# Fused attention and two MoE layers on one core: loading q and k of the first group ahead of need, and adding the mask with a matmul

## The chip, the core and the metric

The kernel runs on one core of a Trainium2 chip. The metric is the device time of one execution in microseconds (us). Five engines work side by side, each through its own instructions in program order: TensorE (PE; its weight loads are listed as PEld), VectorE (DVE), ScalarE (ACT), GpSimd (POOL) and SyncE (SP), which here issues most of the DMA transfers.

## The reference

```python
# attention: 4 batches, 8 heads, 576 positions, 64 channels a head
scores = scale * np.matmul(q, k.transpose(0, 1, 3, 2))
mask_plain = (rel >= 0) & (rel < window)                       # window 32, heads 0-3
mask_dil = (rel >= 0) & (rel < window * dilation) & (rel % dilation == 0)   # dilation 4, heads 4-7
scores = np.where(masks[None, :, :, :], scores, -1000000000.0)
scores = scores - np.max(scores, axis=-1, keepdims=True)
attn = np.exp(scores)
attn = attn / (np.sum(attn, axis=-1, keepdims=True) + 1e-09)
x = np.matmul(attn, v)            # then (4*576, 512) tokens
# first MoE layer, d_ff 2048
h = x @ w_in
y = (h - np.tanh(h)) @ w_out
# second MoE layer, d_ff 1024
h = y @ w_in2
solu = h * softmax(h)
out = (layer_norm(solu) * g_ln) @ w_out2
```

Weights arrive as 64-bit floats, 512 KB for each chunk of 128 rows.

## The kernel before

The 2304 tokens are cut into six groups of 384. Attention for a group is eight *units*; a unit is two heads of two blocks of 96 queries, each against 128 keys. A unit passes through these steps: `qk` (four matmuls into a PSUM tile `qkp`), `then()` of `qk_f32` (DVE adds the mask, takes the row maximum `nm` and writes the masked scores to SBUF as `p`, one instruction for each of four blocks), `sm_exp` (ACT, four exponentials), `sm_norm` (two tiny DVE instructions on the row sums, `rs`, and one POOL multiplication), `tr` (PE transposes `p` into `tp`, ACT copies it to `pt`) and, for two units at a time, `pv` (PE times v; ACT and DVE write the result as a rounded part and a rest, `x`). Units 0 to 21 are computed in full fp32 by `qk_f32`; later units use split operands (`qk_half`) and are not touched.

Each weight chunk is loaded raw (`w_load`) and turned into a rounded part and a rest by `w_step`, a pipeline over four calls: per call one ACT scaling `wa`, one ACT cast `wi`/`wo`, and four DVE instructions (`wi` L85, `wy` L93, L101, L105). There are 32 chunks of the first layer, w_in and w_out.

The program has a *prologue*, rounds r = 0 to 10, for units 0 to 7 of group 0. In round r, PE gets qk of unit r, pv of units r-4 and r-3 (even r), tr of unit r-2; then comes a `w_step` if r is in `SW`, the maximum and exponentials of unit r, the normalisation of unit r-1. Loads are issued by SP in program order; the tile `qkr` that holds q and k of a unit has two buffers, so that the load of unit r+2 waits until PE has read unit r. PSUM tiles `qkp`, `tp` and `pv` have two buffers each in the prologue.

The *main loop* follows: for step s (group g, chunk c of 16), `mm1` computes h in 12 matmuls, tanh, subtraction and split follow on ACT and DVE, and `mm2` adds chunk s-5 to y in 12 matmuls. Attention units of the next groups are put into half-steps (slots) by `plan`: qk of unit u at slot p, its exponentials at slot p+1, its transpose some slots later. They share the PSUM pool `a_ps`, two banks for all of `qkp`, `tp` and `pv` there. `w_step` calls fill the first 42 slots, by the rule with `W0`, `WA`, `WB`. A tile's bank is given to the next tile once all readers of the old one are done. The second layer follows after group 5.

Of the kernel before, what the change touches and what calls it, by code (L numbers as in the profile page):

```python
# [15 lines left out]
B, H, S, D = 4, 8, 576, 64  # L16
# [5 lines left out]
NQ, NK = 96, 128  # L22
NU = 8
QC, KC = 4 * NQ, 4 * NK
# [5 lines left out]
YT = 256  # L30
LAG = 5
WA, WB = 26, 40
SW = range(1, 11)
W0 = 11


@with_exitstack
def tile_kernel(ctx: ExitStack, tc: tile.TileContext, qk, vw, cst, w_in, w_out, w_in2, w_out2, g_ln, out):
    nc = tc.nc
    ctx.enter_context(tc.manual_schedule())  # L40

    const = ctx.enter_context(tc.tile_pool(name="const", bufs=1, side="left"))
    cv_p = ctx.enter_context(tc.tile_pool(name="cv", bufs=2, side="left"))
    wi_p = ctx.enter_context(tc.tile_pool(name="wi", bufs=1, side="left"))
    wo_p = tc.alloc_tile_pool(name="wo", bufs=1, side="left")
    g_p = ctx.enter_context(tc.tile_pool(name="g", bufs=2, side="right"))
    x_p = ctx.enter_context(tc.tile_pool(name="x", bufs=2, side="right"))
    at_p = tc.alloc_tile_pool(name="at", bufs=2, side="right")
# [1 line left out]

    y_dr = dr_p.tile([128, KD, NTOK], F32, name="y_dr")

    cst_sb = const.tile([128, 128 + 3 * NK], F32, name="cst_sb")
    ident = cst_sb[:, 0:128]
    masks = cst_sb[:NQ, 128:].rearrange("p (t k) -> p t k", t=3)

    def mask_of(u, j):

        g, r = divmod(u, NU)
        hp, bp = divmod(r, 2)  # L60
        if hp < 2:
            return 0 if (4 * g + 2 * bp + j) % 6 == 0 else 1
        return (0, 2, 1)[g % 3]
# [46 lines left out]
    wi, wo = [None] * NF, [None] * NF  # L110
# [7 lines left out]


    xt, un = {}, {}  # L120
    NFU = 22

    def load_unit(u):
        if u < NU * NG:
            r = at_p.tile([128, QC + KC], F32, tag="qkr", name=f"qkr{u}")
            n = 64 if u < NFU else 128
            nc.sync.dma_start(out=r[:n], in_=qk[u, :n])
            v = at_p.tile([NK, 2, 2, D], F32, tag="v", name=f"v{u}", bufs=6)
            nc.sync.dma_start(out=v.rearrange("p b h d -> p (b h d)"), in_=vw[u])
            un[u] = dict(r=r, v=v)  # L130

    def prep_unit(u):
        if not NFU <= u < NU * NG:
            return []
        r = un[u]["r"]
        s = at_p.tile([128, QC + 2 * KC], F32R, tag="qks", name=f"qks{u}", bufs=1)
        un[u]["s"] = s
        return [
            lambda: nc.vector.tensor_copy(out=s[:, 0:QC + KC], in_=r),
            lambda: nc.vector.tensor_tensor(out=s[64:128, 0:QC], in0=r[64:128, 0:QC],  # L140
                                            in1=s[64:128, 0:QC].bitcast(F32), op=ALU.subtract),
            lambda: nc.vector.tensor_tensor(out=s[:, QC + KC:], in0=r[:, QC:],
                                            in1=s[:, QC:QC + KC].bitcast(F32), op=ALU.subtract),
        ]

    def new_p(u):
        d = un[u]
        d["p"] = at_p.tile([NQ, 4, NK], F32, tag="p", name=f"p{u}", bufs=3)
        for t in ("nm", "sm", "rs"):
            d[t] = at_p.tile([NQ, 4], F32, tag=t, name=f"{t}{u}")  # L150

    def qk_f32(u, pool, tag):

        d = un[u]
        new_p(u)
        ps = pool.tile([128, 512], F32, tag=tag, name=f"qkp{u}")[:NQ, 0:KC].rearrange("p (b k) -> p b k", b=4)
        for b in range(4):
            nc.tensor.matmul(ps[:, b], d["r"][:64, b * NQ:(b + 1) * NQ],  # L158
                             d["r"][:64, QC + b * NK:QC + (b + 1) * NK], start=True, stop=True)

        def then():
            for b in range(4):
                nc.vector.tensor_tensor_reduce(  # L163
                    out=d["p"][:, b], in0=ps[:, b], in1=masks[:, mask_of(u, b % 2)], op0=ALU.add, op1=ALU.min,
                    scale=-0.125, scalar=3.0e38, accum_out=d["nm"][:, b:b + 1])
        return then

    def qk_half(u, hf, pool, tag):
# [26 lines left out]
    def sm_exp(u, bs=range(4)):  # L195
        d = un[u]
        for b in bs:
            nc.scalar.activation(out=d["p"][:, b], in_=d["p"][:, b], func=AF.Exp, scale=-1.0,  # L198
                                 bias=d["nm"][:, b:b + 1], accum_out=d["sm"][:, b:b + 1])

    def sm_norm(u):
# [42 lines left out]


    st_ps = tc.alloc_tile_pool(name="st_ps", bufs=2, space=PSUM, side="left")
    load_unit(0)
    nc.sync.dma_start(out=cst_sb, in_=cst)
    load_unit(1)
    w_load()  # L250
    load_unit(2)
    for _ in range(3):
        w_load()
    back = None
    for r in range(NU + 3):
        t = qk_f32(r, st_ps, "qk") if r < NU else None
        b1 = pv_pe(r - 4, st_ps, "pv") if r % 2 == 0 and 0 <= r - 4 < NU else None
        b2 = tr_pe(r - 2, st_ps, "tr") if 0 <= r - 2 < NU else None
        if r in SW:
            w_step()  # L260
        if t:
            t()
        if back:
            back()
        back = b1
        if t:
            sm_exp(r)
# [19 lines left out]
    def at(slot, fn):  # L287
        later.setdefault(slot, []).append(fn)
# [272 lines left out]
def _layout(q, k, v, moe_w_in, moe_w_out, moe2_w_in, moe2_w_out, moe2_g_ln):  # L561
    import numpy as np

    def blocks(a, n, back):


        a = np.asarray(a)
        pl = a[:, :H // 2].transpose(1, 0, 2, 3).reshape(H // 2, B * S, D)
        di = a[:, H // 2:].reshape(B, H // 2, S // DIL, DIL, D).transpose(1, 3, 0, 2, 4)
        di = di.reshape(H // 2, DIL, B * S // DIL, D)  # L570
        o = np.zeros((NG, NU, 2, 2, n, D), a.dtype)
        for g in range(NG):
# [24 lines left out]
    qq, kk = np.arange(128)[:, None], np.arange(NK)[None]
    rel = qq + WIN - kk
    ok = (rel >= 0) & (rel < WIN)
    cross = (qq < NQ // 2) == (kk < WIN + NQ // 2)  # L600
    for i, m in enumerate((ok & (kk >= WIN), ok, ok & cross)):
        cst[:, 128 + i * NK:128 + (i + 1) * NK] = np.where(m, 0.0, -8.0e9)
    return dict(
        qk=qkt, vw=vt, cst=cst,
        w_in=bits(moe_w_in).reshape(KD, 128, NF, 128).transpose(2, 1, 0, 3).reshape(NF, 128, 512),
        w_out=bits(moe_w_out).reshape(NF, 128, DM),
        w_in2=bits(moe2_w_in).reshape(KD, 128, 2, 512).transpose(0, 2, 1, 3),
        w_out2=bits(moe2_w_out).reshape(NF2, 128, DM),
        g_ln=np.asarray(moe2_g_ln).reshape(NF2, 128).T,
    )  # L610
# [20 lines left out]
```

## Time and profile before

| | before |
|---|---|
| median of 3 runs | 747.28 us (745.67 to 747.45) |
| the profiled execution | 747.18 us |
| its span, first to last instruction | 745.4 us |
| PE busy | 717.0 us (96%) |
| DVE busy | 490.8 us (66%) |
| ACT busy | 365.5 us (49%) |
| POOL busy | 134.7 us (18%) |
| DMA moved | 63.61 MB, mean 85 GB/s |

The profiled execution takes 1.8 us beyond its span. Busy time is the union of an engine's instructions; a PE that is busy is not for that at its peak. The page's row of the granted TensorE clock shows full speed in nearly every slice; in the first 50 us it must be read together with the duration of the matmuls.

### The profile page before, as it was taken

To read this page: it belongs to the slowest core of one execution; us is meant where nothing else is said; L and a number is where in the kernel's file an instruction comes from. 1 tells how busy PE (TensorE), PEld (TensorE's weight loads), DVE (VectorE), ACT (ScalarE), POOL (GpSimd) and SP (SyncE) were. 2 spreads that over 40 slices of the span, in tenths; PEclk is the share of its full clock that TensorE was granted. 3 is DMA by queue.
4 is the path that set the end of the run, shared out by engine and by line. 5 is a ranking of instruction groups with operands and counts; after the bars stand their busy time and mean duration, and the time that the engine had idled before them with its cause. 6 is when DMAs were issued, how large, how long until landed. Compare 5 with 4: busy or idle time off the path is not lost.

```text
span 745.4 us, 11617 instructions
## 1 busy us (share of the span) xinstructions
PE 717.0 (96%) x4168; PEld 653.4 (88%) x4168; DVE 490.8 (66%) x1273; ACT 365.5 (49%) x991; POOL 134.7 (18%) x187
## 2 busy tenths in 40 slices
PE   4968999999999999999999999999999999999997
PEld 3757899999999999999999999999888888888885
DVE  4889888746777777677777535797465555555452
ACT  4856676543444444354444423453255454535444
POOL 1622243201100111111111000020232312322110
PEclk9998999999999999999999999999999999999999
DMA  8857462122222212232212003733201101110001
GB/s 244 238 206 212 141 200 69 40 90 81 64 63 77 66 63 64 65 106 65 65 64 75 1 1 113 241 113 114 72 14 44 57 28 43 58 42 29 15 29 44
DMA packets 30186, 63.61 MB, mean 85 GB/s; under 512 B 2992, under 2 KB 16816, under 8 KB 30128
## 3 DMA queue, kind: packets, MB, share of 16 engines
q1 hardware_dynamic: 26960, 58.15, 24.8%
q10 hardware_dynamic: 3168, 4.72, 1.8%
q8 instruction: 33, 0.54, 0.3%
q14 instruction: 25, 0.20, 0.1%
HBM read 53.42 MB, written 9.44 MB: 84 GB/s over the span
## 4 chain that ended last, share of the span: by engine, by line
PE 88%; DVE 5%; ACT 3%; DMA 2%; POOL 1%; issue 1%; ACTq 0%; SPq 0%; POOLq 0%; DVEq 0%
PE y L324 26%; PE h L297 24%; PE po L524 14%; PE h L462 14%; PE qkp L158 3%; PE pv L233 2%; PE zt L505 2%; PE tp L212 2%; DMA qkr<-in_qk_dram 2%; PE qkp L178 2%; ACT p L198 1%; POOL p L205 1%; DVE gs L314 1%; DVE wi L85 1%; DVE p L163 1%
## 5 line engine op out<-in xcount | busy, mean ns | idle before, releaser
L297 PE MATMUL h<-x,wi 128*128 128x384 f32 x1152 | 223.5, 344 | 1.9 <-DVE x L242 1.8
L324 PE MATMUL y<-gs,wo 128*128 128x384 f32 x1152 | 217.3, 338 | 0.0
L297 PEld LDWEIGHTS h<-x,wi 128*128 128x128 f32 x1152 | 200.6, 191 | 4.0 <-DVE x L242 2.1
L324 PEld LDWEIGHTS y<-gs,wo 128*128 128x128 f32 x1152 | 198.0, 188 | 2.8
L205 POOL TENSOR_TENSOR p<-p,rs 96x512 f32<-96x512 f32 x48 | 77.8, 1621 | 351.3 <-DVE rs L204 259.0
L462 PE MATMUL h<-w2i,yt 128*128 128x512 f32 x432 | 104.9, 397 | 0.0
L524 PE MATMUL po<-w2o,z 128*128 128x512 f32 x432 | 104.1, 396 | 0.1
L524 PEld LDWEIGHTS po<-w2o,z 128*128 128x128 f32 x432 | 80.7, 188 | 20.4 <-ACT z L513 1.9
L513 ACT ACTIVATE z<-zt,gl_sb 128x128 fp32r<-128x128 f32 x144 | 51.0, 367 | 96.9 <-PE zt L505 48.6
L462 PEld LDWEIGHTS h<-w2i,yt 128*128 128x128 f32 x432 | 79.7, 187 | 18.4
L305 ACT ACTIVATE t<-h 128x384 f32<-128x384 f32 x96 | 47.1, 491 | 96.8 <-PE h L297 90.7
L514 DVE SCALAR_TENSOR_TENSOR z<-zt,gl_sb,z 128x128 fp32r<-128x128 f32 x144 | 48.9, 350 | 69.2 <-ACT z L513 69.2
L198 ACT ACTIVATE p<-p,nm 96x128 f32<-96x128 f32 x192 | 75.0, 392 | 32.8 <-DVE nm L163 32.8
L314 DVE TENSOR_TENSOR gs<-t,gs 128x384 fp32r<-128x384 f32 x96 | 75.7, 788 | 20.9 <-ACT gs L311 18.8
L308 DVE TENSOR_TENSOR t<-h,t 128x384 f32<-128x384 f32 x96 | 52.9, 551 | 32.4 <-ACT t L305 32.4
L311 ACT CAST gs<-t 128x384 fp32r<-128x384 f32 x96 | 49.2, 512 | 47.6 <-DVE t L308 47.5
L158 PE MATMUL qkp<-qkr 64*96 64x128 f32 x176 | 32.5, 340 | 15.6 <-DMA qkr<-in_qk_dram 11.2
L158 PEld LDWEIGHTS qkp<-qkr 64*96 64x96 f32 x176 | 26.7, 206 | 20.7 <-DMA qkr<-in_qk_dram 6.8
L242 DVE TENSOR_TENSOR x<-pv,x 128x384 fp32r<-128x384 f32 x24 | 16.9, 703 | 40.0 <-ACT x L241 40.0
L389 POOL TENSOR_TENSOR yt<-yr,yt 128x1024 fp32r<-128x1024 f32 x9 | 24.3, 2697 | 85.8 <-DVE yt L388 85.8
L479 DVE SCALAR_TENSOR_TENSOR u<-h,e 128x1024 f32<-128x1024 f32 x18 | 22.0, 1225 | 23.9 <-ACT e L478 23.9
L198 ACT ACTIVATION_READ_ACCUMULATOR p<-p,nm 96x1 f32 x192 | 36.2, 188 | 0.0
(68 smaller groups left out, 688.8 us busy)
## 6 DMA issues: line engine op xcount, KB each, us to landing
qkr<-in_qk_dram SPq DMA_DIRECT2D x26, 448.0 KB, 3.3
raw_wi<-in_w_in_dram SPq DMA_DIRECT2D x16, 512.0 KB, 6.4
raw_wo<-in_w_out_dram SPq DMA_DIRECT2D x16, 512.0 KB, 5.4
v<-in_vw_dram SPq DMA_DIRECT2D x48, 128.0 KB, 3.2
qkr<-in_qk_dram SPq DMA_DIRECT2D x22, 224.0 KB, 3.6
y_dr<-ys ACTq DMA_DIRECT2D x6, 768.0 KB, 3.8
yr<-y_dr SPq DMA_DIRECT2D x9, 512.0 KB, 4.4
out_dram<-o SPq DMA_DIRECT2D x18, 256.0 KB, 2.0
```

The source lines that it names most:

```text
L158: nc.tensor.matmul(ps[:, b], d["r"][:64, b * NQ:(b + 1) * NQ], d["r"][:64, QC + b * NK:QC + (b + 1) * NK], start=True, stop=True)
L198: nc.scalar.activation(out=d["p"][:, b], in_=d["p"][:, b], func=AF.Exp, scale=-1.0, bias=d["nm"][:, b:b + 1], accum_out=d["sm"][:, b:b + 1])
L205: nc.gpsimd.tensor_tensor(out=d["p"], in0=d["p"], in1=d["rs"].unsqueeze(2).to_broadcast([NQ, 4, NK]), op=ALU.mult)
L297: nc.tensor.matmul(ps, w[:, a, k * 128:(k + 1) * 128], xt[g, k][:, b], start=(n == 0), stop=(n == 3 * KD - 1))
L308: nc.vector.tensor_tensor(out=t, in0=ps, in1=t, op=ALU.subtract)
L311: nc.scalar.copy(out=gs[:, 0], in_=t)
L314: nc.vector.tensor_tensor(out=gs[:, 1], in0=t, in1=gs[:, 0].bitcast(F32), op=ALU.subtract)
L324: nc.tensor.matmul(yb[g][m], wo[c][:, a, m * 128:(m + 1) * 128], gs[:, b], start=(c == 0 and i == 0), stop=(c == NF - 1 and i == 2))
L462: nc.tensor.matmul(ps[:, n * 512:(n + 1) * 512], y[:, a, k, o:o + TT], w2i[2 * k + n][:, b], start=(q == 0), stop=(q == 3 * KD - 1))
L513: nc.scalar.activation(out=z[:, 0, c], in_=pp[n][:, j], func=AF.Copy, scale=gc)
L514: nc.vector.scalar_tensor_tensor(out=z[:, 1, c], in0=pp[n][:, j], scalar=gc, in1=z[:, 0, c].bitcast(F32), op0=ALU.mult, op1=ALU.subtract)
L524: nc.tensor.matmul(po, z[:, a, j], w2o[j][:, b], start=(q == 0), stop=(q == 3 * NF2 - 1))
```

## The change

- All eight qk tiles of group 0 are loaded at the start into places that chunks 8 to 15 of w_out take later (`wo8` to `wo15`), so none waits for a buffer. They alternate on SP's queue with the v tiles and with five raw chunks instead of four. The constants (identity and masks) come third, behind the first qk tile and the first raw chunk, into a temporary tile, from which DVE casts them to the rounded fp32 format.
- A `w_step` runs in round 0 too, ahead of that unit's maximum; `W0` moves by one with it.
- For units 0 to 21 the mask is no longer added by DVE: a matmul of the identity (96 x 96) with the mask (96 x 512, rounded fp32) starts the accumulation in `qkp`, and the four qk matmuls add to it. The masked value changes from -8.0e9 to -2^33.
- DVE then takes the maximum over all four blocks in one reduction of 96 x 512 out of PSUM and scales it in a second, tiny instruction. The exponentials read `qkp` in PSUM instead of `p` in SBUF.

```diff
-SW = range(1, 11)
-W0 = 11
+SW = range(0, 11)
+W0 = 12
...
+    def load_qk(u):
+        if u < NU:
+            r = wo_p.tile([128, 1024], F32, tag=f"wo{NU + u}", name=f"qkr{u}")[:, 0:QC + KC]
+        else:
+            r = at_p.tile([128, QC + KC], F32, tag="qkr", name=f"qkr{u}")
+        n = 64 if u < NFU else 128
+        nc.sync.dma_start(out=r[:n], in_=qk[u, :n])
+        un[u] = dict(r=r)
...
+        m0, m1 = mask_of(u, 0), mask_of(u, 1)
+        if m0 != m1:
+            ms = rmasks[:, m0:m0 + 2].unsqueeze(1).to_broadcast([NQ, 2, 2, NK])
+        else:
+            ms = rmasks[:, m0:m0 + 1].to_broadcast([NQ, 4, NK])
+        nc.tensor.matmul(ps, cst_sb[:NQ, 0:NQ], ms, start=True, stop=False)
         for b in range(4):
             nc.tensor.matmul(ps[:, b], d["r"][:64, b * NQ:(b + 1) * NQ],
-                             d["r"][:64, QC + b * NK:QC + (b + 1) * NK], start=True, stop=True)
+                             d["r"][:64, QC + b * NK:QC + (b + 1) * NK], start=False, stop=(b == 3))
+        d["sc"] = ps
 
         def then():
-            for b in range(4):
-                nc.vector.tensor_tensor_reduce(
-                    out=d["p"][:, b], in0=ps[:, b], in1=masks[:, mask_of(u, b % 2)], op0=ALU.add, op1=ALU.min,
-                    scale=-0.125, scalar=3.0e38, accum_out=d["nm"][:, b:b + 1])
+            nc.vector.tensor_reduce(out=d["nm"], in_=ps, axis=mybir.AxisListType.X, op=ALU.max, negate=True)
+            nc.vector.tensor_scalar(out=d["nm"], in0=d["nm"], scalar1=0.125, scalar2=None, op0=ALU.mult)
...
         for b in bs:
-            nc.scalar.activation(out=d["p"][:, b], in_=d["p"][:, b], func=AF.Exp, scale=-1.0,
+            src, sc = (d["sc"], 0.125) if "sc" in d else (d["p"], -1.0)
+            nc.scalar.activation(out=d["p"][:, b], in_=src[:, b], func=AF.Exp, scale=sc,
                                  bias=d["nm"][:, b:b + 1], accum_out=d["sm"][:, b:b + 1])
...
-    load_unit(0)
-    nc.sync.dma_start(out=cst_sb, in_=cst)
-    load_unit(1)
+    load_qk(0)
     w_load()
-    load_unit(2)
-    for _ in range(3):
-        w_load()
+    cst_f = g_p.tile([128, 128 + 3 * NK], F32, tag="ys", name="cst_f", bufs=1)
+    nc.sync.dma_start(out=cst_f, in_=cst)
+    nc.vector.tensor_copy(out=cst_sb, in_=cst_f)
+    for u in range(1, NU):
+        load_qk(u)
+        if u <= 6:
+            load_v(u - 1)
+        if u <= 4:
+            w_load()
...
-        if r + 3 < NU + 2:
-            load_unit(r + 3)
+        if r in (4, 5):
+            load_v(r + 2)
+        if r in (6, 8):
+            load_unit(NU + r // 2 - 3)
```

At the start of the program SP's queue of loads stands as follows before the change (`qkr` is q and k of a unit, `v` its values, `raw_wi` a raw chunk of w_in; 224, 128 and 512 KB; `cst` is 256 KB):

```order
L127 DMA qkr0_86<-in_qk_dram 64x896
L129 DMA v0_88<-in_vw_dram 128x256
L248 DMA cst_sb_81<-in_cst_dram 128x512
L127 DMA qkr1_91<-in_qk_dram 64x896
L129 DMA v1_93<-in_vw_dram 128x256
L78 DMA raw_wi0_95<-in_w_in_dram 128x1024
L127 DMA qkr2_97<-in_qk_dram 64x896
L129 DMA v2_99<-in_vw_dram 128x256
L78 DMA raw_wi1_101<-in_w_in_dram 128x1024
```

and in the changed program:

```order
L130 DMA qkr0_86<-in_qk_dram 64x896
L80 DMA raw_wi0_88<-in_w_in_dram 128x1024
L269 DMA cst_f_90<-in_cst_dram 128x512
L130 DMA qkr1_93<-in_qk_dram 64x896
L135 DMA v0_95<-in_vw_dram 128x256
L80 DMA raw_wi1_97<-in_w_in_dram 128x1024
L130 DMA qkr2_99<-in_qk_dram 64x896
L135 DMA v1_101<-in_vw_dram 128x256
L80 DMA raw_wi2_103<-in_w_in_dram 128x1024
L130 DMA qkr3_105<-in_qk_dram 64x896
```

The constants stand behind 736 KB instead of 352 KB, and no load up to that of v of unit 6 waits for a buffer.

PE's first rounds in the changed program, with what the instructions wait for (96x512 is the product with the mask, 96x128 the qk matmuls, `tp` the transposes):

```order
L175 MATMUL qkp0_131<-cst_sb_81 96x512 [waits DVE_49]
L177 MATMUL qkp0_131<-qkr0_86 96x128 [waits DMAHW0_49]
L177 MATMUL qkp0_131<-qkr0_86 96x128 x3
L175 MATMUL qkp1_154<-cst_sb_81 96x512
L177 MATMUL qkp1_154<-qkr1_93 96x128 [waits DMAHW3_49]
L177 MATMUL qkp1_154<-qkr1_93 96x128 x3
L175 MATMUL qkp2_181<-cst_sb_81 96x512 [waits DVE_49,Activation_49]
L177 MATMUL qkp2_181<-qkr2_99 96x128 [waits DMAHW6_49]
L177 MATMUL qkp2_181<-qkr2_99 96x128 x3
L231 MATMUL tp0_187<-cst_sb_81,p0_127 128x96 [waits Pool_49]
```

A new row stands ahead of each unit's four. The first waits for DVE's cast of the constants, and from unit 2 on the new row waits for ACT as well as DVE, since the exponentials of unit r-2 are the last readers of that PSUM buffer.

PE's rows in the main loop around unit 10, before the change:

```order
L212 MATMUL tp8_712<-cst_sb_81,p8_566 128x96 [waits Pool_49]
L212 MATMUL tp8_712<-cst_sb_81,p8_566 128x96 [waits Activation_49] x3
L158 MATMUL qkp10_722<-qkr10_598 96x128 [waits DMAHW7_49,DVE_49]
L158 MATMUL qkp10_722<-qkr10_598 96x128 x3
L297 MATMUL h5_758<-x0_0_248,wi5_448 128x384 [waits DVE_49]
```

and after it:

```order
L231 MATMUL tp8_717<-cst_sb_81,p8_573 128x96 [waits Pool_49]
L231 MATMUL tp8_717<-cst_sb_81,p8_573 128x96 x3
L175 MATMUL qkp10_727<-cst_sb_81 96x512 [waits DVE_49,Activation_49]
L177 MATMUL qkp10_727<-qkr10_604 96x128 [waits DMAHW1_49]
L177 MATMUL qkp10_727<-qkr10_604 96x128 x3
L322 MATMUL h5_762<-x0_0_260,wi5_412 128x384 [waits DVE_49]
```

Unit 10 takes the bank of unit 9. It waited for DVE, the maximum of unit 9; now it waits for ACT, the exponentials of unit 9. The same holds for the transpose of unit 11, which takes the bank of unit 12.

## Rows read from the trace of the kernel before

**Rows 1.** Busy time by stretch (us): PE, PEld, DVE, ACT, POOL, PEclk, DMA share, GB/s.

```profile
0.00:20.00 20.00, 8.82 (x37) 7.34 (x37) 7.78 (x36) 8.88 (x30) 3.50 (x6) 1.00 0.87 246
20.00:35.00 15.00, 14.25 (x81) 11.57 (x80) 13.50 (x57) 13.20 (x46) 11.00 (x4) 1.00 0.83 240
35.00:47.40 12.40, 6.00 (x45) 4.29 (x44) 10.86 (x28) 8.73 (x22) 6.10 (x3) 1.00 0.92 335
47.40:92.00 44.60, 39.58 (x220) 36.45 (x221) 40.95 (x115) 29.36 (x85) 7.77 (x4) 0.92 0.50 151
92.00:150.00 58.00, 58.00 (x388) 54.35 (x387) 46.59 (x140) 37.79 (x109) 20.44 (x8) 1.00 0.34 99
150.00:450.00 300.00, 299.22 (x1977) 289.91 (x1977) 201.72 (x558) 132.34 (x400) 29.21 (x28) 1.00 0.20 63
450.00:730.00 280.00, 279.98 (x1382) 241.46 (x1380) 164.99 (x329) 127.78 (x284) 55.73 (x132) 1.00 0.20 67
```

**Rows 2.** Pieces of the chain that ended last, first 50 us (start, length, what).

```profile
2.44 5.96 DMA qkr<-in_qk_dram
...
10.49 7.41 DMA qkr<-in_qk_dram
...
40.32 2.85 POOL p L205
...
47.42 4.22 PE h L297 x12
```

**Rows 3.** Timeline of the prologue, rounds 3 to 5, and DVE at round 7.

```profile
20.17 0.29 DVE L163 CUSTOM_DVE_ANT_0 p<-qkp,cst_sb 96x128 f32<-96x128 f32 x1 [2.32 <-PE qkp L158]
...
20.56 0.40 ACT L198 ACTIVATE p<-p,nm 96x128 f32<-96x128 f32 x1 [1.96 <-DVE nm L163]
...
21.02 1.99 PE L158 MATMUL qkp<-qkr 64*96 64x128 f32 x8 [0.17 <-DVE nm L163]
...
21.53 2.87 POOL L205 TENSOR_TENSOR p<-p,rs 96x512 f32<-96x512 f32 x1 [2.78 <-ACT p L198]
...
22.94 1.55 PE L233 MATMUL pv<-pt,v 128*64 128x96 f32 x16
...
24.46 0.90 PE L212 MATMUL tp<-cst_sb,p 96*128 96x96 f32 x4
...
25.29 2.02 PE L158 MATMUL qkp<-qkr 64*96 64x128 f32 x8
...
35.21 0.29 DVE L163 CUSTOM_DVE_ANT_0 p<-qkp,cst_sb 96x128 f32<-96x128 f32 x1 [0.70 <-PE qkp L158]
```

**Rows 4.** Timeline of PE in the main loop, 60 to 92 us.

```profile
67.23 2.02 PE L158 MATMUL qkp<-qkr 64*96 64x128 f32 x8 [3.62 <-DVE nm L163]
69.17 4.04 PE L297 MATMUL h<-x,wi 128*128 128x384 f32 x12
...
75.49 2.25 PE L297 MATMUL h<-x,wi 128*128 128x384 f32 x12
...
88.28 0.52 PE L212 MATMUL tp<-cst_sb,p 96*128 96x96 f32 x4 [0.66 <-POOL p L205]
...
91.55 1.11 PE L158 MATMUL qkp<-qkr 64*96 64x128 f32 x8 [0.64 <-ACT pt L218]
```

**Rows 5.** Timeline: arrival of the constants and of the first raw chunk.

```profile
6.80 0.29 DVE L163 CUSTOM_DVE_ANT_0 p<-qkp,cst_sb 96x128 f32<-96x128 f32 x1 [6.80 <-DMA cst_sb<-in_cst_dram]
...
10.25 0.67 ACT L92 ACTIVATE wa_wi<-raw_wi 128x512 f32<-128x512 f32 x1 [1.47 <-DMA raw_wi<-in_w_in_dram]
```

**Rows 6.** Groups by line: busy us, mean ns of one, idle before.

```profile
L462 PE MATMUL h<-w2i,yt 128*128 128x512 f32 x432 | 104.9, 397 | 0.0
...
L477 DVE TENSOR_REDUCE sml<-h 128x1 f32<-128x1024 f32 x18 | 22.0, 1221 | 9.4 <-PE h L462 9.4
...
L163 DVE CUSTOM_DVE_ANT_0 p<-qkp,cst_sb 96x128 f32<-96x128 f32 x88 | 20.1, 282 | 12.6 <-DMA cst_sb<-in_cst_dram 6.8 <-PE qkp L158 5.8
...
L480 DVE TENSOR_SCALAR sml<-sml 128x1 f32<-128x1 f32 x18 | 2.8, 154 | 0.6
```

**Rows 7.** Timeline of ACT, the last exponential of unit 9.

```profile
67.80 0.39 ACT L198 ACTIVATE p<-p,nm 96x128 f32<-96x128 f32 x1
```

**Rows 8.** Timeline of DVE behind the maximum of unit 9, and of unit 11.

```profile
68.71 0.56 DVE L314 TENSOR_TENSOR gs<-t,gs 128x384 fp32r<-128x384 f32 x1 [1.07 <-ACT gs L311]
...
84.33 0.56 DVE L314 TENSOR_TENSOR gs<-t,gs 128x384 fp32r<-128x384 f32 x1 [1.10 <-ACT gs L311]
```

**Rows 9.** Groups by line from 92 us to the end, PE alone.

```profile
L158 PE MATMUL qkp<-qkr 64*96 64x128 f32 x71 | 9.8, 278 | 0.0
```

More of the change, by code (lines that the diff above doesn't have):

```diff
@@ L51, in tile_kernel @@
     y_dr = dr_p.tile([128, KD, NTOK], F32, name="y_dr")
-    cst_sb = const.tile([128, 128 + 3 * NK], F32, name="cst_sb")
-    ident = cst_sb[:, 0:128]
-    masks = cst_sb[:NQ, 128:].rearrange("p (t k) -> p t k", t=3)
+    cst_sb = const.tile([128, 128 + 3 * NK], F32R, name="cst_sb")
+    ident = cst_sb[:, 0:128].bitcast(F32)
+    rmasks = cst_sb[:NQ, 128:].rearrange("p (t k) -> p t k", t=3)
+    masks = cst_sb[:NQ, 128:].bitcast(F32).rearrange("p (t k) -> p t k", t=3)
     def mask_of(u, j):
@@ L120, in tile_kernel, with load_v @@
     xt, un = {}, {}
+    def load_qk(u):
[6 more added lines that the diff above has]
+        un[u] = dict(r=r)
+    def load_v(u):
+        v = at_p.tile([NK, 2, 2, D], F32, tag="v", name=f"v{u}", bufs=6)
+        nc.sync.dma_start(out=v.rearrange("p b h d -> p (b h d)"), in_=vw[u])
+        un[u]["v"] = v
     NFU = 22
@@ L124, in load_unit @@
         if u < NU * NG:
[L125 to L130, printed above, removed]
+            load_qk(u)
+            load_v(u)
     def prep_unit(u):
@@ L246, in tile_kernel @@
     st_ps = tc.alloc_tile_pool(name="st_ps", bufs=2, space=PSUM, side="left")
-    load_unit(0)
-    nc.sync.dma_start(out=cst_sb, in_=cst)
-    load_unit(1)
+    load_qk(0)
     w_load()
-    load_unit(2)
-    for _ in range(3):
-        w_load()
+    cst_f = g_p.tile([128, 128 + 3 * NK], F32, tag="ys", name="cst_f", bufs=1)
+    nc.sync.dma_start(out=cst_f, in_=cst)
+    nc.vector.tensor_copy(out=cst_sb, in_=cst_f)
+    for u in range(1, NU):
+        load_qk(u)
+        if u <= 6:
+            load_v(u - 1)
+        if u <= 4:
+            w_load()
     back = None
@@ L601, in _layout @@
     for i, m in enumerate((ok & (kk >= WIN), ok, ok & cross)):
-        cst[:, 128 + i * NK:128 + (i + 1) * NK] = np.where(m, 0.0, -8.0e9)
+        cst[:, 128 + i * NK:128 + (i + 1) * NK] = np.where(m, 0.0, -2.0 ** 33)
     return dict(
```

## The prediction

> **What bounds the kernel now.** I read the busy time by stretch first. From 92 us to 730 us PE is busy without a gap (58.00 of 58, 299.22 of 300, 279.98 of 280 us): whatever PE gets there in addition is paid in full, and nothing that other engines save there is worth anything [rows 1]. All of PE's idle time that could be won lies before 92 us: about 18 us in the prologue (to 47.4 us) and 5 us in the stretch from 47.4 to 92 us.
>
> The chain of waits shows that the prologue's start is paced by loads: two pieces of 5.96 and 7.41 us wait for q and k of units 1 and 3. Its end is paced by a ring over engines, of which a piece of POOL's multiplication of unit 7 (40.32 us) is the last; h starts at 47.42 us [rows 2]. Between them the timeline shows PE with hardly a gap: from 21.02 us qk, pv, transposes and qk follow each other, and over the stretch from 20 to 35 us PE is busy for 14.25 of 15 us [rows 1, 3]. The granted clock reads 1.00 there, but the pace is that of the lower level (1.2 GHz): a unit's qk takes 2.0 us, and the first 12 matmuls of h take 4.22 us [rows 2, 3]; later the same qk takes 1.11 and the 12 matmuls 2.25 us [rows 4], the upper level (2.4 GHz). So the rounds from 20 us on are close to bound by PE at its lower clock, no longer by loads.
>
> From 47.4 to 92 us DVE is busy for 40.95 of 44.6 us [rows 1]. It works off weight splits, and PE waits for it: 3.62 us before qk of unit 10 at 67.23 us. After that wait the clock is at the lower level (h takes 4.04 us). Two short waits of 0.66 and 0.64 us follow at 88.28 and 91.55 us [rows 4].
>
> **The change part by part.** The sum is made against the profiled execution, 747.18 us, 1.8 us of it outside its span; the median of the runs is 747.28 us, so no correction is needed.
>
> *The loads.* Bytes stay the same, apart from one more raw chunk up front; only order and issue time move. The two waits for q and k go. What comes in their place: the constants now have 384 KB more ahead of them, and the first PE instruction waits for them, where before only DVE did, until 6.80 us [rows 5]. At the 240 to 335 GB/s of the prologue's stretches 384 KB are 1.2 to 1.6 us [rows 1]; the queue isn't full that early, so I take 0.7 us, with 0 and 1.6 as bounds. DVE's cast of 128x512 is an estimate of 0.4 us, below half of the 1.22 us of a 128x1024 reduction [rows 6]. PE starts at about 8.0 us. The raw chunk that round 0 now splits is there by then (it ended waits at 10.25 us when three loads more were ahead of it [rows 5]).
>
> *The mask product in the prologue.* No row shows 512 columns at the lower clock. 12 matmuls of 384 columns take 4.22 us [rows 2], so 512 columns are 4.22 / 12 x 512 / 384 = 0.47 us; the bound below is the same at the upper clock, 104.9 us / 432 = 0.24 us [rows 6]. A unit's qk becomes 2.0 + 0.47 = 2.47 us.
>
> *PE's schedule.* Units 0 to 2: 8.0 + 3 x 2.47 = 15.4 us. The first transpose waits for unit 0's multiplication on POOL, which comes behind unit 1's maximum (qk of unit 1 ends at 12.9; maximum, normaliser and hand-overs 1.4 us more) and takes up to 2.87 us [rows 3]; I take 2, and PE goes on at 16.4 us. From there to the end of unit 7's qk it has five transposes of 0.90, five qk of 2.47 and two pv of 1.55 us [rows 3]: 20.0 us without any gap, so 36.4 us. Before, DVE took unit 7 over at 35.21 us [rows 3], so its qk ended at 35.1: 1.3 us later. The shorter work of DVE per unit (below) gives back 0.1, and part of the end is held by POOL alone. I put the start of h **1.0 us later**. Bounds: with the constants at 6.8 us and no gap before the first transpose 1 us earlier than before; with the late constants and POOL at its longest 2.5 us later. The exponentials also start later: they followed DVE's start by 0.39 us, one block at a time [rows 3]; now they need the whole reduction. That is an estimate of 0.61 us, half of 1.221, plus the tiny instruction of 0.154 us [rows 6] and hand-overs: 0.95 us, 0.55 more. DVE itself is relieved: 20.1 us / 22 units = 0.91 us become 0.76 [rows 6].
>
> *The stretch from 47.4 to 92 us.* The number of weight splits in each slot is the same, since `W0` moved with `SW`; the one split fewer falls off the end, where PE is the bound and it is worth nothing. But now the bank of unit 9 is free only after its exponentials. The last of them ended at 68.19 us [rows 7], when qk of unit 10 had been running for a microsecond. It starts 0.55 us later in its own right, and what waits behind exponentials on ACT (the cast of gs, for which DVE sat idle for 1.07 and 1.10 us [rows 8]) shifts likewise, unit 8's by some 0.4. So unit 10 goes from 67.23 to about 69.1 us: +1.9. Its product costs 0.47 at the lower clock, those of units 11 and 12 0.24 each: +0.95. Queued behind on PE are h, transposes and y. The later waits of 0.66 and 0.64 us [rows 4] take up some of the delay, but the transpose of unit 11 now waits for the exponentials of unit 12, which start 0.55 us later too; I let 0.85 be taken up. Sum: **2.0 us later** at unit 13, over and above the prologue; bounds 0 (all of it covered by the old waits) and 3.5 us (none, and a longer spell of the lower clock).
>
> *The products from 92 us on.* 71 recorded instructions, eight to a unit, are nine units [rows 9]. 9 x 0.24 = **2.2 us**, with PE never idle there [rows 1]. If idle gaps hid it it would be 0, but there are none.
>
> Reading the exponentials from PSUM, and the casts of the other tiles, I cost at nothing: ACT is busy for 29.36 of 44.6 us in the tight stretch and less later [rows 1].
>
> Sum: 747.18 + 1.0 + 2.0 + 2.2 = 752.4 us.
>
> **The clock as a rule.** The rows first: PE had no gap from 21.02 to 27.3 us, and the qk at 25.29 us still took 2.02 us; h rose to the upper pace within its first 12 matmuls or soon after, both at 47.42 and at 69.17 us [rows 2, 3, 4]. Small matmuls of 64 rows, pv and transposes thus did not raise the clock here; matmuls of h did. The Trainium skill (TensorE: Matmul & The Clock Gate, Part 1) says that the throttled state is the default and that activity releases it. By that rule a prologue without gaps should come up to the full clock. The trace agrees for h and not for qk. With the sum as above it is 752.4 us; by the rule it is the first rival.
>
> **The rivals.**
> - *The denser PE gets the upper clock in the prologue.* Each product of 512 columns adds dense work to each round. Then DVE paces the rounds: it is busy for 13.50 of 15 us [rows 1], so 1.4 us come off this stretch; transposes and pv at the end of the prologue lose 1.2, and the first 12 of h take 2.25 instead of 4.22 us: -4.6. With 2.0 + 2.2 that is 746.8 us. Against it stands the row at 25.29 us [rows 3].
> - *The loads pay more than I reckon.* If the constants arrive early and POOL's first multiplications are short, the prologue is 1 us shorter; with the new wait before unit 10 mostly covered (+0.5) that is 747.18 - 1.0 + 0.5 + 2.2 = 748.9 us. It decides by h's start: before 46.5 us.
> - *Faster: DVE catches up.* In the loop PE loses 3.62 us before unit 10 and, at the lower clock behind it, 2.02 - 1.11 + 4.04 - 2.25 = 2.7 us [rows 4]. If lighter maxima let unit 9's exponentials end before PE comes to unit 10, both vanish: 747.18 + 1.0 - 6.3 + 0.7 (products of units 10 to 12) + 2.2 = 744.8 us. It decides at the point where the exponentials end by 63.6 us instead of 68.19, which needs 4.6 us; two maxima save 0.3.
>
> **How the numbers follow.** The forecast has a chance of 0.67 (750 to 755.5 us), the well-paying loads 0.14, the clock 0.12, DVE catching up 0.07. About 0.3%, or 2.2 us, is what a measurement of this kernel can tell from no change: faster is below 745.0, slower above 749.5 us. The forecast is slower but for 0.03; the loads' case is mostly the same; the clock's case same or faster; the last faster or just the same. That makes 0.68 slower, 0.21 same, 0.11 faster. The range from 745.5 to 755.5 us leaves out the case of DVE catching up, part of the clock's, and a prologue and a stretch both at their late bounds.
>
> **What would show it.** Right: h starts at 48 to 49 us; PE in the prologue without gaps between 17 and 36 us, qk at 2.0 us and the product at 0.47; the first matmul of unit 10 waiting for ACT, starting later after h's start than now; DVE's reduction near 0.6 us; from there to the end the profile of before, longer by the products. Wrong: qk at 1.1 us before h starts, which would make the prologue's term negative; a product that costs much less than 0.24 us beside y and h; unit 10 without a wait.

## The result, and the profile after

The changed kernel takes 751.93 us (median of 4 runs, 751.74 to 752.63); the kernel before took 746.89 us beside it (745.67 to 747.45). The ratio is 1.0068, 95% interval 1.0054 to 1.0081: slower by 5 us. The profiled execution took 751.86 us, with a span of 749.7 us against 745.4 before.

The busy time by stretch, in the columns of [rows 1]:

```profile
0.00:20.00 20.00, 11.99 (x45) 8.97 (x45) 10.42 (x25) 9.47 (x32) 5.32 (x6) 1.00 0.94 265
20.00:35.00 15.00, 14.95 (x81) 11.72 (x80) 12.68 (x32) 12.15 (x46) 11.20 (x4) 1.00 1.00 347
35.00:47.40 12.40, 6.15 (x46) 4.28 (x44) 10.76 (x22) 8.82 (x22) 5.90 (x3) 1.00 0.82 271
47.40:92.00 44.60, 37.63 (x211) 34.00 (x212) 39.26 (x81) 26.59 (x81) 7.76 (x4) 0.92 0.43 140
92.00:150.00 58.00, 58.00 (x382) 53.38 (x381) 43.42 (x94) 34.51 (x102) 19.39 (x7) 1.00 0.28 81
150.00:450.00 300.00, 299.22 (x1978) 289.71 (x1978) 201.81 (x546) 133.73 (x409) 30.20 (x29) 1.00 0.20 64
450.00:730.00 280.00, 280.00 (x1386) 242.88 (x1385) 164.80 (x327) 127.51 (x282) 55.60 (x132) 1.00 0.20 67
```

The loads do what they are there for: in the second stretch DMA goes from 240 to 347 GB/s, and no wait for q or k is left in the chain. PE fills that stretch (14.95 of 15 us). From 47.4 to 92 us PE does less than before, 37.63 us instead of 39.58. From 92 us on it is as full as it was.

Two pieces of the chain that ended last, where [rows 2] had two waits for q and k:

```profile
1.97 4.47 DMA cst_f<-in_cst_dram
...
40.31 2.85 POOL p L224
```

The timeline of PE (L175 is the product with the mask, L177 qk, L231 tp, L322 h):

```profile
6.95 0.74 PE L175 MATMUL qkp<-cst_sb 96*96 96x512 f32 x1 [6.95 <-DVE cst_sb L270]
7.62 2.02 PE L177 MATMUL qkp<-qkr 64*96 64x128 f32 x8
...
15.93 0.90 PE L231 MATMUL tp<-cst_sb,p 96*128 96x96 f32 x4 [1.03 <-POOL p L224]
...
25.19 2.02 PE L177 MATMUL qkp<-qkr 64*96 64x128 f32 x8
...
47.41 4.85 PE L322 MATMUL h<-x,wi 128*128 128x384 f32 x18 [1.83 <-DVE x L261]
...
68.82 0.74 PE L175 MATMUL qkp<-cst_sb 96*96 96x512 f32 x1 [5.18 <-ACT p L217]
69.49 2.02 PE L177 MATMUL qkp<-qkr 64*96 64x128 f32 x8
71.44 3.75 PE L322 MATMUL h<-x,wi 128*128 128x384 f32 x12
...
91.39 0.52 PE L231 MATMUL tp<-cst_sb,p 96*128 96x96 f32 x4 [1.33 <-issue]
...
93.86 0.40 PE L175 MATMUL qkp<-cst_sb 96*96 96x512 f32 x1
```

The timelines of DVE and ACT: arrival of the constants, and unit 9 (L182 maximum, L183 scaling, L217 exponentials):

```profile
6.46 0.43 DVE L270 CAST cst_sb<-cst_f 128x512 fp32r<-128x512 f32 x1 [6.46 <-DMA cst_f<-in_cst_dram]
...
66.28 0.67 DVE L182 TENSOR_REDUCE nm<-qkp 96x4 f32<-96x512 f32 x1
66.99 0.17 DVE L183 TENSOR_SCALAR nm<-nm 96x4 f32<-96x4 f32 x1
67.07 0.55 DVE L333 TENSOR_TENSOR t<-h,t 128x384 f32<-128x384 f32 x1
...
69.20 0.56 DVE L339 TENSOR_TENSOR gs<-t,gs 128x384 fp32r<-128x384 f32 x1 [1.58 <-ACT gs L336]
```

```profile
67.27 0.36 ACT L217 ACTIVATE p<-qkp,nm 96x128 f32<-96x128 f32 x1 [2.46 <-DVE nm L183]
...
68.31 0.36 ACT L217 ACTIVATE p<-qkp,nm 96x128 f32<-96x128 f32 x1
...
90.84 0.36 ACT L217 ACTIVATE p<-qkp,nm 96x128 f32<-96x128 f32 x1
```

Three points cut the span into three terms: the start of h, the first instruction of unit 13 (in [rows 4] the qk at 91.55 us), and the end. Before, they lie at 47.42, 91.55 and 745.4 us; after at 47.41, 93.86 and 749.7 us. So the prologue is 0.0 us longer, the stretch up to unit 13 is 46.45 us instead of 44.13 (**+2.3**), and the rest 655.84 us instead of 653.85 (**+2.0**). The sum, 4.3 us, is the difference of the spans. Outside its span the changed kernel spends 2.2 us, the kernel before 1.8, which makes 4.7 us between the two profiled executions. No experiment explains these 0.4 us; every run of the changed kernel, e5, e6 and e9 has them (2.10 to 2.22 us outside the span) and no run of the others (1.74 to 1.87).

The stretch is where the reading pays. Unit 10 waits 5.18 us for ACT where it waited 3.62 us for DVE [rows 4], and ACT's last exponential of unit 9 ends at 68.67 us, just ahead of the product. The transpose of unit 11 waits twice as long as before (1.33 instead of 0.66 us); the row says "issue", and the exponentials of unit 12, whose bank it takes, end at 91.2 us, just ahead of it.

### The profile page after: what moved, and what is told of

It is laid out like the page before. It is cut to its first block, busy times and chain, and to the rows that moved or that the text cites. A ratio compares the mean times of both kernels' runs of the same rounds, so it can differ in the third digit from the quotient of the medians.

```text
span 749.7 us, 11521 instructions
## 1 busy us (share of the span) xinstructions
PE 723.7 (97%) x4190; PEld 656.3 (88%) x4190; DVE 489.6 (65%) x1142; ACT 361.3 (48%) x991; POOL 136.3 (18%) x187
## 4 chain that ended last, share of the span: by engine, by line
PE 91%; DVE 4%; ACT 2%; POOL 1%; issue 1%; DMA 1%; ACTq 0%; SPq 0%; POOLq 0%
PE y L349 26%; PE h L322 25%; PE po L549 14%; PE h L487 13%; PE qkp L177 3%; PE pv L252 2%; PE tp L231 2%; PE zt L530 2%; PE qkp L196 2%; POOL p L224 1%; PE qkp L175 1%; DMA cst_f<-in_cst_dram 1%; ACT p L217 1%; DVE nm L182 0%; DVE gs L339 0%
## 5 line engine op out<-in xcount | busy, mean ns | idle before, releaser
L322 PE MATMUL h<-x,wi 128*128 128x384 f32 x1152 | 222.4, 343 | 2.3 <-DVE x L261 1.8
L322 PEld LDWEIGHTS h<-x,wi 128*128 128x128 f32 x1152 | 199.5, 191 | 4.4 <-DVE x L261 2.1
L224 POOL TENSOR_TENSOR p<-p,rs 96x512 f32<-96x512 f32 x48 | 79.6, 1658 | 354.2 <-DVE rs L223 258.8
L217 ACT ACTIVATE p<-qkp,nm 96x128 f32<-96x128 f32 x88 | 30.8, 357 | 40.9 <-DVE nm L183 34.4
L217 ACT ACTIVATE p<-p,nm 96x128 f32<-96x128 f32 x104 | 40.7, 393 | 0.0
L177 PEld LDWEIGHTS qkp<-qkr 64*96 64x96 f32 x176 | 26.7, 206 | 8.1 <-issue 8.1
L177 PE MATMUL qkp<-qkr 64*96 64x128 f32 x176 | 32.6, 341 | 0.0
```

The lines of the kernel that those rows point to most:

```text
L217: nc.scalar.activation(out=d["p"][:, b], in_=src[:, b], func=AF.Exp, scale=sc, bias=d["nm"][:, b:b + 1], accum_out=d["sm"][:, b:b + 1])
L224: nc.gpsimd.tensor_tensor(out=d["p"], in0=d["p"], in1=d["rs"].unsqueeze(2).to_broadcast([NQ, 4, NK]), op=ALU.mult)
L322: nc.tensor.matmul(ps, w[:, a, k * 128:(k + 1) * 128], xt[g, k][:, b], start=(n == 0), stop=(n == 3 * KD - 1))
```

## The experiments

The three terms of every run, read in the same way from its profile (us; span and terms are of the profiled execution, the median of all runs):

| run | median | start of h | h to unit 13 | unit 13 to end | span |
|---|---|---|---|---|---|
| before | 746.89 | 47.42 | 44.13 | 653.85 | 745.4 |
| after | 751.93 | 47.41 | 46.45 | 655.84 | 749.7 |
| e1 loads | 746.10 | 48.74 | 44.06 | 653.80 | 746.6 |
| e2 product | 754.54 | 50.28 | 46.63 | 655.89 | 752.8 |
| e3 product up to unit 7 | 746.68 | 47.46 | 43.89 | 653.55 | 744.9 |
| e4 DVE frees the bank | 749.50 | 47.59 | 43.65 | 656.06 | 747.3 |
| e5 no product | 748.87 | 45.77 | 46.97 | 653.46 | 746.2 |
| e6 dense start | 751.90 | 47.01 | 46.88 | 655.91 | 749.8 |
| e7 loads, dense start | 745.45 | 45.72 | 44.06 | 653.72 | 743.5 |
| e8 loads, no split in round 0 | 743.30 | 43.29 | 44.06 | 653.75 | 741.1 |
| e9 all, no split in round 0 | 752.88 | 48.06 | 46.86 | 655.88 | 750.8 |
| e10 as e8, dense start | 743.12 | 43.43 | 44.10 | 653.77 | 741.3 |

The last two terms take only two sizes each, whatever the prologue does: 43.65 to 44.13 or 46.45 to 46.97 us, and 653.46 to 653.85 or 655.84 to 656.06 us.

### The two parts apart: e1 and e2

e1 keeps the loads and the split in round 0; mask, maximum and exponentials are as before. Two pieces of its edit, against the changed kernel:

```diff
-        nc.tensor.matmul(ps, cst_sb[:NQ, 0:NQ], ms, start=True, stop=False)
...
-            nc.vector.tensor_reduce(out=d["nm"], in_=ps, axis=mybir.AxisListType.X, op=ALU.max, negate=True)
+            for b in range(4):
+                nc.vector.tensor_tensor_reduce(
```

> The new loads and the split in round 0, with the mask and the maximum on DVE as before, no product on PE. Theory (in the prologue PE at its lower clock took up what the loads gave, with eight products of 0.43 to 0.67 us): PE is spared some 4 us before h, h starts 1 to 3 us before 47.4, and the loop is as before, so 744 to 746 us. Rival (the prologue's end is held by the ring of maximum, normaliser, POOL and transpose, whatever the loads and PE do): h at 47.4 us again and 747 us.

746.10 us (12 runs, 745.18 to 748.84); ratio 0.999 (0.998 to 1.0). With the split in round 0 the loads move next to nothing, between the theory's 744 to 746 us and the rival's 747. The profiled execution, 748.43 us, is one of the two long ones: there DVE waited for raw chunks five times, 12.0 us in all (5.2 of them for the first), and h started at 48.74 us. The other two terms are those of before.

e2 keeps the loads of before and `SW`, `W0` too, and changes the rest. Its edit, against the changed kernel (pieces):

```diff
-    load_qk(0)
-    w_load()
...
+    load_unit(0)
```

> The mask product, the whole maximum and the exponentials from PSUM, with loads, split rounds and W0 as before. Theory: products of the units from 18 us on add to PE's gapless rounds, h starts 1.5 to 2.5 us later than 47.4, and the loop loses its 4.3 us: 753 to 754 us. Rival (ring of POOL holds the prologue): h at 47.4, 751.5 us.

754.54 us; ratio 1.0098 (1.0085 to 1.0112). Unit 3 waits for its load in the timeline of PE of e2:

```profile
19.93 2.02 PE L165 MATMUL qkp<-qkr 64*96 64x128 f32 x8 [2.65 <-DMA qkr<-in_qk_dram]
```

h starts 2.9 us later than before, and both later terms are those of the whole change. Start and time lie a little beyond the theory (1.5 to 2.5 us, 753 to 754 us); the rival's 751.5 us is out. With products, then, the new loads and the split together are worth 754.54 - 751.93 = 2.6 us.

### The loop: e3, e4, e5

e3 has the product for units 0 to 7 alone; from unit 8 on DVE adds the mask.

```diff
-    def qk_f32(u, pool, tag):
+    def qk_prod(u, pool, tag):
...
+    def qk_f32(u, pool, tag):
+        if u < NU:
+            return qk_prod(u, pool, tag)
```

> The changed kernel with the product for units 0 to 7 alone; units 8 to 21 get mask and maximum on DVE as before. Theory (the loss lies wholly in the loop, in products and the later release of banks): h at 47.4 us, unit 10 at 67.2 us, 747 us, the same as before. Rival (the split moved into round 0 or the raw chunks that come in another order cost time in the loop): above 749 us.

746.68 us; ratio 1.0003 (0.9994 to 1.0011). The timeline of PE of e3:

```profile
67.07 1.11 PE L194 MATMUL qkp<-qkr 64*96 64x128 f32 x8 [3.60 <-DVE nm L199]
...
91.35 1.11 PE L194 MATMUL qkp<-qkr 64*96 64x128 f32 x8 [0.62 <-ACT pt L255]
```

The whole loss is gone, with a prologue that starts h at 47.46 us: it lay in the loop. Unit 10 waits for DVE again, and the wait before unit 13 is back.

e4 keeps every product, but DVE reads the bank as before and writes `p` (the mask is added a second time), and the exponentials read `p`. A bank is free after the maximum again.

```diff
-        d["sc"] = ps
...
-            nc.vector.tensor_reduce(out=d["nm"], in_=ps, axis=mybir.AxisListType.X, op=ALU.max, negate=True)
+            for b in range(4):
+                nc.vector.tensor_tensor_reduce(
```

> The changed kernel with the product on PE, but DVE takes the maximum in four pieces as before, adds the mask a second time and writes p to SBUF, so that DVE frees the bank and the exponentials start after the first piece. Theory (in the stretch to unit 13 the later exponentials and the later release cost 2.3 us, mostly; the products only 0.5 to 1): unit 10 at about 67.3 us, products cost 2.0 from 92 us on, 749.5 to 750.3 us. Rival (the stretch is lost to the products on PE): 751.5 us.

749.50 us; ratio 1.0033 (1.0021 to 1.0045). Unit 10 in the timeline of PE of e4:

```profile
67.01 0.44 PE L175 MATMUL qkp<-cst_sb 96*96 96x512 f32 x1 [3.60 <-DVE nm L182]
67.38 1.73 PE L177 MATMUL qkp<-qkr 64*96 64x128 f32 x8
```

It waits 3.60 us for DVE, as before, and the loss up to unit 13 is gone (43.65 us), with the products of units 10 to 12 still in it. The 2.2 us from unit 13 on stay.

e5 leaves the mask out altogether and keeps the one maximum and the exponentials out of PSUM.

```diff
-        nc.tensor.matmul(ps, cst_sb[:NQ, 0:NQ], ms, start=True, stop=False)
...
-                             d["r"][:64, QC + b * NK:QC + (b + 1) * NK], start=False, stop=(b == 3))
+                             d["r"][:64, QC + b * NK:QC + (b + 1) * NK], start=True, stop=True)
```

> The changed kernel without the products: the mask of units 0 to 21 is left out altogether, the one reduction and the exponentials from PSUM stay. Theory (the stretch to unit 13 is lost to the later release of the banks and the later exponentials, the rest of the loop to the products alone): PE waits some 5 us for ACT before unit 10, unit 13 starts 2 us later after the start of h than before, nothing is lost from there on; with h 0 to 1 us earlier 748 to 749.5 us. Rival (the products are the loss in the stretch too): 746 to 747 us.

748.87 us; ratio 1.0035 (1.0021 to 1.0049). The timeline of PE of e5:

```profile
67.57 2.02 PE L171 MATMUL qkp<-qkr 64*96 64x128 f32 x8 [5.19 <-ACT p L211]
...
90.17 0.52 PE L225 MATMUL tp<-cst_sb,p 96*128 96x96 f32 x4 [1.54 <-issue]
```

This is the mirror image: without a product in the program unit 10 waits 5.19 us for ACT and the stretch is 46.97 us; from unit 13 on nothing is lost. h starts 1.65 us earlier than before, where 0 to 1 us was expected, so beside the split the products cost the prologue 1.6 us. e4 and e5 show the two terms apart: the stretch belongs to maximum and exponentials, the rest to the products. Within the stretch e4 puts back two things at once, the bank that DVE frees and the exponentials that start after the first piece; no run parts them. The rows of the changed kernel give an estimate: the reduction of unit 9 is done with the bank at 66.95 us, the exponentials at 68.67, so 1.7 us of the wait hang on who reads the bank last.

### The prologue: e8 and e9

e8 is e1 without the split in round 0.

```diff
-SW = range(0, 11)
-W0 = 12
+SW = range(1, 11)
+W0 = 11
```

> The new loads alone, and no weight split in round 0 (SW and W0 as before). Theory: the early loads are worth about 1 us without products, whether or not round 0 splits a chunk: 745.5 to 746.5 us. Rival (the split in round 0 delays the first maximum and takes up the gain): 744 to 745 us.

743.30 us; ratio 0.9955 (0.9943 to 0.9968): faster than both kernels. My theory here, that the loads are worth little with or without that split, fell; the time is even below the rival's 744 to 745 us. h starts 4.1 us earlier than before. The timeline of PE of e8:

```profile
43.29 1.97 PE L313 MATMUL h<-x,wi 128*128 128x384 f32 x5 [1.83 <-DVE x L254]
...
63.07 1.11 PE L170 MATMUL qkp<-qkr 64*96 64x128 f32 x8 [3.61 <-DVE nm L175]
```

With the split DVE needs each raw chunk a round earlier, ahead of that round's maximum, and the chunk isn't there. In e7 (below, the loads with the split) the chain runs through it:

```profile
3.60 5.45 DMA raw_wi<-in_w_in_dram
...
9.41 0.69 DVE wy_wi L102
10.10 0.60 DVE wy_wi L106
10.70 0.20 DVE p L175
```

The maximum of unit 1 stands behind the split of the second chunk, which landed at 9.05 us. DVE never waits for a raw chunk in e8's prologue.

e9 is the whole change with the same edit.

> The whole change, but with no weight split in round 0 (SW and W0 as before). In the loads alone this one edit was worth 2.8 us. Theory: with the products PE paces the prologue (busy without a gap from 15.9 to 36 us at the lower clock), and the split of round 0 lies in DVE's idle time before the first maximum; taking it out gives nothing. h starts at 47 to 47.6 us and the time is 751 to 752.5 us, ratio 1.006 to 1.007 of before. Rival: the split costs the same with and without the products, since it makes DVE need each raw chunk a round earlier; then h starts at 43.5 to 45 us and the time is 748 to 749.5 us.

752.88 us; ratio 1.0082 (1.0068 to 1.0095). Nothing is won, but the theory's figures are missed too: h starts at 48.06 us, 0.65 us later than in the changed kernel, and the time is above 752.5 us. One reason is in the timeline of ACT of e9:

```profile
10.69 1.28 ACT L217 ACT_TABLE_LOAD   x1 [10.69 <-DVE nm L183]
11.98 0.36 ACT L217 ACTIVATE p<-qkp,nm 96x128 f32<-96x128 f32 x1
```

The load of ACT's table lies behind the wait for the maximum, and the chain that ended last runs through it. In the changed kernel the same 1.28 us lie at 0.72 us, ahead of the first `wa` of round 0. In e9 PE waits for the exponentials behind it at the product of unit 2, and for POOL, further down the same chain, before the second transpose, as its timeline shows:

```profile
13.53 0.74 PE L175 MATMUL qkp<-cst_sb 96*96 96x512 f32 x1 [1.23 <-ACT p L217]
...
19.89 0.90 PE L231 MATMUL tp<-cst_sb,p 96*128 96x96 f32 x4 [0.47 <-POOL p L224]
```

The Trainium skill (ScalarE: Activation LUTs, What ACT_TABLE_LOAD costs) gives 1283 ns for such a load; the trace agrees with 1.28 us.

What decides the place of this load isn't shown. In e9 and in e2 (10.49 us) the first activation is an exponential out of PSUM. In e8, and in the kernel before, it is an exponential too and waits for a maximum, but it reads SBUF, and the load lies ahead of the wait, as in the timeline of ACT of e8:

```profile
0.72 1.28 ACT L210 ACT_TABLE_LOAD   x1 [0.72 <-PEq L635]
6.71 0.40 ACT L210 ACTIVATE p<-p,nm 96x128 f32<-96x128 f32 x1 [4.71 <-DVE nm L175]
```

So e9 took away the split and moved the table's load with one edit. Without PE's two waits, 1.70 us together, h would start at 46.4 us at the earliest (an estimate from the two rows). The rival's 43.5 to 45 us is out, but that the split costs nothing with the products is not shown: at most 1.0 us, by this estimate.

Without products the loads and no split bring h 4.1 us forward (e8); with the products it is 4.8 us later than that (e9), of which up to 1.7 us belong to the late table. With the split it is 45.72 us (e7), 48.74 us (e1, in one of its two long runs) or 47.41 us (after). So the products use up at least 3.1 of the 4.1 us, and the split without products costs 2.8 us by the medians (e1 against e8).

### The clock: e6, e7, e10

Twelve bf16 matmuls of 128x512 stand ahead of the first product of the changed kernel in e6; nine ahead of qk in e7 (as e1) and in e10 (as e8).

```diff
+    for _ in range(12):
+        nc.tensor.matmul(wps, wm[:, 0:128], wm[:, 128:640], start=True, stop=True)
```

> The changed kernel with 12 matmuls of 128x512 on constants ahead of the first product, while PE waits for loads; nobody reads them. Theory: PE at its lower clock sets the prologue's pace. If the small matmuls hold a clock that dense ones have raised, qk takes 1.1 us and h starts 1 to 3 us earlier: 749 to 751 us. If they don't hold it, the clock is back at the lower level within the first rounds and nothing changes: 751.5 to 752.5 us. Rival (PE doesn't bound the prologue): h at 47.4 us even where qk takes 1.1 us.

751.90 us; ratio 1.0075 (1.0063 to 1.0088). The timeline of PE of e6:

```profile
1.41 5.30 PE L271 MATMUL wps<-wm 128*128 128x512 bf16 x12 [1.41 <-POOL wm L268]
...
7.37 1.11 PE L177 MATMUL qkp<-qkr 64*96 64x128 f32 x8
...
8.82 1.11 PE L177 MATMUL qkp<-qkr 64*96 64x128 f32 x8
11.05 0.74 PE L175 MATMUL qkp<-cst_sb 96*96 96x512 f32 x1 [1.12 <-ACT p L217]
11.72 2.02 PE L177 MATMUL qkp<-qkr 64*96 64x128 f32 x8
```

Two units run at the upper level (2.4 GHz), and from the third on qk takes 2.02 us again, at the lower one. h starts 0.4 us earlier, and the stretch behind it gives that back.

> The kernel with the new loads alone (mask on DVE) and 9 such matmuls ahead of the first qk. If the clock holds: qk at 1.1 us, the ring of maximum, POOL, transpose and qk shorter by some 1.3 us a turn of two rounds, h 2 to 4 us earlier: 742 to 744 us. If it falls back: 745.5 to 746.5 us as with the loads alone.

745.45 us (11 runs, 744.89 to 749.72); ratio 0.999 (0.9976 to 1.0005). The same picture: qk of units 0 and 1 takes 1.76 and 1.11 us, and 1.99 us or more from unit 2 on. No gain over e1 can be told.

> The loads alone without the split of round 0 (743.3 us), and nine dense matmuls of 128x512 ahead of the first qk. Theory: they bring units 0 and 1 to a qk of 1.1 us and no more, as in the two runs with a dense start before; POOL's ring of about 3.6 us a round then starts 0.5 to 1 us earlier, h at 42.3 to 42.8 us, and the time is 742.3 to 742.8 us. Rival 1: the ring is held by the arrival of q and k of unit 1 and of raw chunks, so that nothing comes of it: 743.3 us. Rival 2: the dense start holds the clock now that fewer splits lie between, qk of units 2 to 7 at 1.1 us, h at 40 us or earlier: below 741 us.

743.12 us; ratio 0.9951 (0.9938 to 0.9965). Nothing comes of it beside e8's 743.30 us, as rival 1 said; PE now waits 1.98 us for q and k of unit 2 instead. It does show how the granted clock is to be read. First the stretch from 20 to 35 us of e8, then of e10:

```profile
20.00:35.00 15.00, 12.82 (x74) 9.93 (x72) 13.46 (x54) 12.97 (x46) 10.88 (x5) 1.00 1.04 352
```

```profile
20.00:35.00 15.00, 13.13 (x80) 10.16 (x76) 13.26 (x53) 12.95 (x45) 10.49 (x4) 0.50 1.04 346
```

Both run qk in 2.02 us there. The row reads 1.00 in the one and 0.50 in the other. Of e10's five runs three have a mean granted clock of 0.968 to 0.972 and two of 0.995, at the same times (742.97 to 743.15 us).

## Why the prediction held, step by step

**The loads and the start of PE.** Mis-sized. I put the constants 0.7 us later, for 384 KB more ahead of them; they came 0.34 us earlier, at 6.46 instead of 6.80 us [rows 5], just outside my bounds of 0 and 1.6 us later. In both programs they are the third transfer, issued at 1.97 us, and 384 KB more ahead of them make no difference that shows: behind 736 KB they are there at 6.30 to 6.51 us (after, e3, e4, e5, e6, e9), behind 352 KB at 6.80 (before) and 6.31 us (e2). PE started at 6.95 us, not 8.0, and the first transpose stood at 15.93 us, not 16.4.

**The product in the prologue.** Right in size for most units: 0.47 forecast; between transposes and qk of units 4 to 7 it adds 0.43 us (from a transpose's start to that of the instruction behind qk, 3.21 us with the product, from 23.93 us on, and 2.78 in e8 without, from 13.04 us on). In units 0 to 2, without a transpose ahead, it takes 0.67 us; they took 7.9 us, not 7.4, and the wait of 1.03 us before the first transpose absorbed it. PE is gapless from 15.93 us until qk of unit 7 ends, as forecast, at about 35.2 instead of 36.4 us.

**The sum of the prologue.** +1.0 forecast, 0.0 measured. Unit 7's qk ends 1.2 us ahead of the forecast: 0.5 of it lies ahead of the first transpose, and 0.7 behind it, where I added durations although one instruction starts before the last has ended (19.3 us measured, 20.0 forecast). So it ends where it did before, POOL's last multiplication starts at 40.31 instead of 40.32 us [rows 2], and h follows it. What I did not see is that the split in round 0 costs time of its own: "the raw chunk is there by then" holds for the first chunk (5.46 us; four loads more stood ahead of it before, not three) and not for the later ones. Without products it costs 2.8 us (e1 against e8); with them at most 1.0 us by the estimate above, since PE, full from 15.93 us on, paced the rounds.

**The stretch to unit 13.** +2.0 forecast, +2.3 measured, and by the steps named. The exponentials of unit 9 start 0.64 us later (67.27 against 66.63 us before; forecast 0.55) and unit 10's bank comes free with them: its h goes from 69.17 us [rows 4] to 71.44, +2.27. h takes 0.29 us less, the products of units 11 and 12 add 0.46, the transpose of unit 11 waits 0.67 us longer: 3.11 us by 91.39 us. The wait of 0.64 us before unit 13 [rows 4] takes up most of what is given back. In the terms of the forecast: unit 10 starts 1.59 us later (1.9 forecast), the products cost 1.13 (0.95; 0.67 of it at unit 10, where 0.47 was put), and 0.4 us is taken up (0.85). e4 and e5 show the cause.

**The products from 92 us on.** 2.2 forecast, 2.0 measured. The group of the product from 92 us on, busy time and mean ns:

```profile
L175 PE MATMUL qkp<-cst_sb 96*96 96x512 f32 x9 | 3.7, 408 | 0.0
```

The 408 ns overlap with what follows: from a product's start to that of its qk it is 0.33 us, and the step ahead of it is 0.10 us shorter (at unit 11 from h's start to the product 2.08 us, before to the qk 2.18). Nine times 0.23 is 2.1 us. e2, e4, e6 and e9 have this term, 655.88 to 656.06 us; e3 and e5 don't, 653.46 and 653.55 us.

**DVE.** Its reduction was put at 0.61 us and takes 0.68, the scaling 0.19 (estimate 0.154; means of 22). At unit 9 the instruction behind the maximum starts 0.79 us after it (66.28 to 67.07), before 0.85 us (66.25 to 67.10): 0.06 us saved, not 0.15. That is less than what DVE waits longer for ACT: 1.58 us ahead of gs, behind unit 9's maximum, where it was 1.07 [rows 8].

**The rivals.** The upper clock in the prologue did not come (qk 2.02 us throughout), and e6 shows that a dense start does not keep it. The loads' case was decided by h before 46.5 us; it came at 47.41. Its gain exists, 4.1 us in e8, but not beside the products and the split. DVE catching up needed the exponentials of unit 9 to end by 63.6 us; they ended at 68.67.

**The whole.** +5.2 us forecast, +5.0 measured between the medians. The two later terms came as forecast, by their steps. That the sum is this near is luck in part: the prologue's term was 1.0 us too large, and 0.3 us more in the stretch and the 0.4 us outside the span, which no term had, stand against it.

**What stays open.** The 0.4 us outside the span; why two of the eleven or twelve runs each of e1, e3 and e7 lie 2.2 to 4.3 us above their median; what puts the table's load behind the wait in e2 and e9; and what lets PE fall to the lower level at the third unit of e6.

## What to carry to other kernels

Where few PSUM banks are shared, ask of each edit who reads the bank last: one maximum over all blocks and exponentials out of PSUM, instead of out of a copy in SBUF, cost 2.3 to 2.8 us here, since ACT was done with the bank later than DVE. Work put on the engine that is full from there to the end is paid by the instruction, however small, so it has to be bought with waits that end last. And of a change with several edits, try each alone: the loads by themselves, with the split left where it was, are 0.45% faster than the kernel before (e8).

## What the runs showed of the hardware

- A granted clock of 1.00 is no proof of the upper level. From 20 to 35 us it read 1.00 in a run whose PE had no dense start and 0.50 in one that had, at the same qk of 2.02 us. The duration of a known matmul is the safer reading.
- A dense start raised PE to the upper level by the first unit (qk 1.11 us), but it fell back at the third, after an idle time of 1.12 us, and stayed there though PE was then busy for 14.90 of 15 us (20 to 35 us of e6). The Trainium skill (TensorE: Matmul & The Clock Gate, Part 1) says that activity releases the throttle; the trace agrees for the dense start (qk 1.11 us behind it) and not for the rounds of qk, product, pv and transposes behind that (2.02 us).
- Exponentials of 96x128 read from PSUM take 0.36 us, those from SBUF 0.39 [rows 7].
- The load of ACT's table, 1.28 us, lay at 0.72 us, hidden, in the kernel before, the changed kernel and e8, and at 10.5 to 10.7 us, behind the wait for the maximum, in e2 and e9, whose first activation reads PSUM; there PE waited 1.23 us for the exponentials behind it.
